# Fourteen products of the identity ahead of the first transposes

## The chip, the cores and the metric

The kernel runs on one core of one Trainium2 chip. The core has a matrix engine (TensorE, in the profile PE, with its weight loads as PEld), a vector engine (DVE), a scalar engine (ACT), a third engine for elementwise work (POOL) and an engine that only issues transfers (SP). They run side by side, each through its own list of instructions in order, and wait for each other by semaphores. The metric is the device time of one execution in microseconds (us). Lower is better.

## What is computed

Attention with normalised q and k, and behind it an MLP mixer. All data are float32. Batch 8, 12 heads, sequence 448, head dimension 64. The heads side by side make 768 channels.

```python
def rmsnorm(x, g):
    return x / np.sqrt(np.mean(x * x, axis=-1, keepdims=True) + 1e-06) * g

q_n, k_n = rmsnorm(q, g_q), rmsnorm(k, g_k)
scores = np.matmul(q_n, k_n.transpose(0, 1, 3, 2)) / np.sqrt(64)
attn = softmax(scores)                                # over the last axis
x = np.matmul(attn, v)                                # to (batch, seq, 768)

h = np.maximum(x.transpose(0, 2, 1) @ w_tok1, 0.0) @ w_tok2
u = x + h.transpose(0, 2, 1)                          # mixing along the sequence, 448 -> 256 -> 448
out = u + np.maximum(u @ w_ch1, 0.0) @ w_ch2          # mixing along the channels, 768 -> 1536 -> 768
```

## The kernel before

**Staging.** Heads are handled in pairs, six pairs to a batch, 48 in all. For a pair, q and k are loaded with the sequence on the partitions, squared on ACT (`square`, L1429), summed on DVE (`reduce`, L1445), the inverse root is found by Newton steps (`guess`, `newton`, L1467 to L1488), and DVE multiplies it in (`scale`, L1496). For the first pairs PE then turns q and k, so that the head dimension lies on the partitions (`turn_qk`, L429, a product with the identity as one operand), and ACT copies the turned blocks out of PSUM (L437 for k, L435 for q, which multiplies the gains in). `score` forms the scores of two pairs at a time (L455) and ACT takes their exponentials (L459). `values` multiplies with v (L528) and sums the rows with a matrix of ones (L508). Then follow, for each batch, the token mixing (L839, L846, L881) and the channel mixing (L971, L1001, L1050, L1067), for which the float weights are converted and combined on the chip (`weight_load` L222 and the conversions L345 to L379).

**Order.** Nothing is reordered by a scheduler: all engines have the order in which the program is written. Attention of a batch is interleaved with the mixing of the batch before it by lists of work items (`merge`, `place`, `run`).

**Start.** The class `Start` issues the loads of the first pairs, makes the identity on POOL (L1344, a memset and a select), normalises pairs 0 and 1, and decides on DVE, from the gains, whether the scores can get large (`large`, L1337). Then every engine loads that one number and takes a branch (L1533). Each arm of the branch holds the whole rest of the kernel, `whole`, once with shifted exponentials and once without; with these inputs it is the second. `whole` sets up its pools, issues loads of v, of weights and of pairs 4 and 5 on SP (L1204 to L1214), squares pairs 2 and 3 on ACT, and turns q and k of pairs 0 and 1: 16 transposes on PE in four groups, each group in a PSUM tile of its own.

**PSUM.** `ps_S` is a ring of four banks; `s_tile` takes the next. Turned blocks, scores and some sums use it. A tile waits until the tile four before it has been read. The identity `ident` is a 128x128 tile in `const`, which also serves later transposes.

The part of `whole` that orders the start:

```python
    pre.square(2, st)
    for p in range(2):
        for i in (1, 0):
            turn_qk(p, i)
        if not p:
            pre.square(3, st)
```

Of the kernel before, what the change touches and what calls it, by code (L numbers as in the profile page):

```python
# [83 lines left out]
def whole(ctx, tc, shifted, pre, q, k, v, g_q, g_k, moe_w_tok1, moe_w_tok2, moe_w_ch1, moe_w_ch2, out):  # L84


    nc = tc.nc
# [7 lines left out]
    P = 128  # L95
# [46 lines left out]
    ident, one_c, expo_c, g_t = pre.ident, pre.one_c, pre.expo_c, pre.g_t  # L142
# [9 lines left out]
    st = dict(pre.st)  # L152
    m_tile = lambda: ps_M.tile([P, 512], F32, name="m_ps", tag="M")
    s_tile = lambda name: ps_S.tile([P, 512], F32, name=name, tag="S")

    clock, pending = [0.0], []

# [1348 lines left out]
def kernel(  # L1506
# [26 lines left out]
    with tc.If(nc.values_load(large[0:1, 0:1], min_val=0, max_val=1,  # L1533
                              skip_runtime_bounds_check_because="a comparison's result") > 0) as arm:
        whole(tc, True, pre, *args)
    with arm.Else():
        whole(tc, False, pre, *args)
# [30 lines left out]
```

## Time and profile before

| | us |
|---|---|
| median of 3 runs | 1285.12 (1283.40 to 1287.99) |
| the profiled execution | 1283.78 |
| its span, first to last instruction | 1282.0 |
| PE busy | 1251.6 (98%) |
| DVE busy | 795.3 (62%) |
| ACT busy | 393.3 (31%) |
| POOL busy | 387.9 (30%) |
| PE before its first product | 12.77 |
| PE's longest later gap, at 28.15 | 3.27 |

All times in the profile count from the start of the span. A group of instructions has a line of the kernel, an engine, what is written and what is read, and a count. PE's products are pipelined, so one of them lasts longer than the step from one to the next. "PEldq", "ACTq" and so on are the sequencers of the engines, which take branches and semaphore waits; a wait's own record tells how long the sequencer stood in it. The releaser of an idle time is what ended it.

### The profile page before, as it was taken

How to read it: one execution, taken by the hardware profiler on the slowest of the kernel's cores; microseconds unless marked ns; L12 is line 12 of the kernel's file. 1: busy time of each engine (PE TensorE's matmuls, PEld its weight loads, DVE VectorE, ACT ScalarE, POOL GpSimd, SP SyncE). 2: the span in 40 equal slices, each digit the busy share in tenths (PEclk: the TensorE clock that was granted, in tenths of full speed). 3: DMA queues.
4: the chain of work that ended last, by engine and by line, in shares of the span. 5: the costliest groups of instructions: out<-in, count | busy, mean ns of one | idle time of the engine just before them, and what ended most of it. 6: DMA issues, size and time to landing. Idle time of an engine off the chain costs nothing.

```text
span 1282.0 us, 20022 instructions
## 1 busy us (share of the span) xinstructions
PE 1251.6 (98%) x7236; PEld 890.8 (69%) x7236; DVE 795.3 (62%) x1241; ACT 393.3 (31%) x785; POOL 387.9 (30%) x629
## 2 busy tenths in 40 slices
PE   4999999999999999999999999999999999999998
PEld 3444444457744487796778768885887867797998
DVE  6989778856664255864668356765558456554243
ACT  5663433223341144302443033311343024300210
POOL 1202552024995611331133122241122322131222
PEclk9999999999999999999999999999999999999999
DMA  7866595899899876695657867595766864386554
GB/s 174 192 188 175 154 233 147 208 241 250 239 237 229 195 165 169 142 249 117 159 161 160 207 142 185 131 222 123 190 159 141 236 134 138 115 208 146 185 175 103
DMA packets 490112, 228.37 MB, mean 178 GB/s; under 512 B 371860, under 2 KB 450580, under 8 KB 490004
## 3 DMA queue, kind: packets, MB, share of 16 engines
q1 hardware_dynamic: 483394, 214.25, 67.9%
q0 software_dynamic: 3584, 12.06, 3.1%
q8 instruction: 59, 0.97, 0.3%
q10 hardware_dynamic: 3026, 0.69, 0.3%
q14 instruction: 49, 0.40, 0.1%
HBM read 184.26 MB, written 42.66 MB: 177 GB/s over the span
## 4 chain that ended last, share of the span: by engine, by line
PE 86%; DVE 6%; DMA 2%; SPq 2%; issue 1%; ACT 1%; DVEq 0%; ACTq 0%
PE m_ps L1001 26%; PE m_ps L1067 21%; PE s_ps L455 9%; PE o_ps L528 8%; PE m_ps L881 5%; PE m_ps L971 5%; PE m_ps L1050 4%; PE m_ps L839 2%; PE t_ps L839 2%; PE d_ps L508 1%; DVE raw L346 1%; DVE raw L348 1%; DVE stage L379 1%; DMA raw<-wp 1%; PE m_ps L846 1%
## 5 line engine op out<-in xcount | busy, mean ns | idle before, releaser
L1067 PE MATMUL m_ps<-hb,unit 128*128 128x224 f32 x1440 | 277.2, 354 | 0.0
L1067 PEld LDWEIGHTS m_ps<-hb,unit 128*128 128x128 f32 x1440 | 270.9, 190 | 8.8 <-issue 7.7
L1001 PE MATMUL m_ps<-tu,unit 128*128 128x224 f32 x1008 | 201.6, 355 | 1.3 <-ACT r L1011 1.3
L1001 PEld LDWEIGHTS m_ps<-tu,unit 128*128 128x128 f32 x1008 | 189.1, 190 | 15.1 <-issue 9.2
L459 ACT ACTIVATE e<-s_ps 128x448 f32<-128x448 f32 x294 | 138.1, 549 | 177.7 <-PE s_ps L455 169.4
L1001 PE MATMUL m_ps<-uT,unit 128*128 128x224 f32 x756 | 151.2, 354 | 0.5 <-DVE hb L1007 0.5
L1001 PEld LDWEIGHTS m_ps<-uT,unit 128*128 128x128 f32 x756 | 142.2, 190 | 7.6 <-issue 4.6
L455 PE MATMUL s_ps<-qkT 64*64 64x448 f32 x1260 | 143.7, 545 | 0.8 <-ACT x L821 0.8
L528 PE MATMUL o_ps<-e,v 64*64 64x448 f32 x1148 | 129.4, 538 | 0.3 <-ACT uT L565 0.2
L496 DVE TENSOR_TENSOR es<-es,e 128x896 f32<-128x896 f32 x90 | 103.5, 1150 | 13.0 <-ACT e L459 7.6
L1007 DVE TENSOR_TENSOR hb<-m_ps,r 128x448 f32<-128x448 f32 x63 | 39.1, 621 | 108.5 <-POOL r L1007 57.0
L1007 POOL TENSOR_TENSOR hb<-r,r 128x448 f32<-128x448 f32 x21 | 24.0, 1143 | 243.6 <-ACT r L1023 243.6
L455 PEld LDWEIGHTS s_ps<-qkT 64*64 64x64 f32 x1260 | 44.9, 132 | 70.0 <-issue 59.9
L528 PEld LDWEIGHTS o_ps<-e,v 64*64 64x64 f32 x1148 | 45.2, 133 | 62.9 <-issue 59.2
L1475 POOL TENSOR_TENSOR nt<-rs 128x56 f32<-128x56 f32 (+1 forms) x54 | 21.9, 405 | 203.5 <-DVE rs L1467 200.7
L1008 ACT ACTIVATE hb<-hb 128x448 f32<-128x448 f32 x84 | 48.4, 577 | 101.1 <-DVE hb L1007 77.6
L881 PE MATMUL m_ps<-w_sb,h 128*128 128x448 f32 x192 | 75.2, 544 | 0.3 <-DVE uT L886 0.3
L1082 POOL TENSOR_TENSOR uT<-uT,r 128x448 f32<-128x448 f32 x42 | 51.4, 1240 | 78.5 <-DVE r L1082 46.7
L320 POOL TENSOR_TENSOR raw<-raw 128x128 f32<-128x128 f32 x128 | 64.4, 522 | 34.3 <-DMA raw<-wp 29.8
L1445 DVE TENSOR_REDUCE ms<-sq 128x28 f32<-128x896 f32 (+2 forms) x44 | 47.5, 1080 | 35.6 <-ACT sq L1432 28.6
L1007 DVE TENSOR_TENSOR r<-m_ps,r 128x448 f32<-128x448 f32 x42 | 26.1, 622 | 64.3 <-PE m_ps L1001 64.3
L886 DVE TENSOR_TENSOR uT<-uT,m_ps 128x448 f32<-128x448 f32 x48 | 29.3, 613 | 54.5 <-PE m_ps L881 54.5
(146 smaller groups left out, 1600.2 us busy)
## 6 DMA issues: line engine op xcount, KB each, us to landing
unit<-ws SPq DMA_DIRECT2D x267, 384.0 KB, 4.2
raw<-in_moe_w_ch_dram SPq DMA_DIRECT2D x72, 256.0 KB, 3.4
v<-in_v_dram SPq DMA_DIRECT2D x96, 112.0 KB, 3.9
out_dram<-turned SPq DMA_DIRECT2D x182, 56.0 KB, 1.9
xs<-xt SPq DMA_DIRECT2D x56, 168.0 KB, 4.7
qk_t<-in_q_dram SPq DMA_DIRECT2D x144, 56.0 KB, 3.5
qk_t<-in_k_dram SPq DMA_DIRECT2D x144, 56.0 KB, 3.7
x<-xs SPq DMA_DIRECT2D x42, 192.0 KB, 3.9
```

The lines of the kernel that those rows point to most:

```text
L320: nc.gpsimd.tensor_tensor(out=at[o], in0=at[x], in1=at[y], op=ALU.add if op == "+" else ALU.subtract)
L455: nc.tensor.matmul(out=pss[i][rows_of(i, a), 0:S], lhsT=qkT[h, 1, k * D:(k + 1) * D], rhs=qkT[h, 0, :], start=True, stop=True)
L459: nc.scalar.activation(out=e[:, i, :], in_=pss[i][:, 0:S], func=AF.Exp)
L496: nc.vector.tensor_tensor(out=es[:], in0=(es if k > 1 else st["e", t, 0])[:], in1=st["e", t, k][:], op=ALU.add)
L528: nc.tensor.matmul(out=st["o", p][a * D:(a + 1) * D, 0:S], lhsT=vt[rows, k * D:(k + 1) * D], rhs=e[rows, :], **kw)
L839: nc.tensor.matmul(out=st["t1", h][jc][:, 0:HC], lhsT=w1_sb[:, c, jc * P:(jc + 1) * P], rhs=st["x", b, h][:, :, c, :], start=start and c = ...
L881: nc.tensor.matmul(out=ps[:, 0:S], lhsT=st["h1", jc][:, cc * P:(cc + 1) * P], rhs=w2_sb[:, jc].rearrange("p c r -> p (c r)"), start=(jc == ...
L971: nc.tensor.matmul(out=ps, lhsT=a[:, o + 2 * half, :], rhs=natural(half * KF + t) if wide else u[:, half * KC + t, :], start=(t == 0 and h ...
L1001: nc.tensor.matmul(out=ps[:, j * HS:(j + 1) * HS], lhsT=w[:, t, j, :], rhs=m, start=(t == 0), stop=(t == KC - 1))
L1007: add = lambda e, o, x, y: e.tensor_tensor(out=o, in0=x, in1=y, op=ALU.add)
L1067: nc.tensor.matmul(out=ps[:, x * HS:(x + 1) * HS], lhsT=st["w"][:, tile_at % 6, :], rhs=hb[:, X_SLOT[f], i, :], start=(i == 0), stop=(i == 3))
L1082: e.tensor_tensor(out=get(out), in0=get(x_), in1=get(y), op=ALU.add if op == "+" else ALU.subtract)
```

## The change

In `whole`, right after the two PSUM helpers are defined, a tile of the ring `ps_S` is taken, and 14 products of the identity with itself are written into its first 128 columns. Each begins and ends its own sum, so each overwrites the one before. Nothing reads the tile. The products stand on PE behind the branch and in front of the first transposes; every later tile of the ring is one bank further on.

```diff
     m_tile = lambda: ps_M.tile([P, 512], F32, name="m_ps", tag="M")
     s_tile = lambda name: ps_S.tile([P, 512], F32, name=name, tag="S")
+
+    first_ps = s_tile("first_ps")
+    for _ in range(14):
+        nc.tensor.matmul(out=first_ps[:, 0:P], lhsT=ident[:, :], rhs=ident[:, :], start=True, stop=True)
 
     clock, pending = [0.0], []
```

Line numbers below the insertion are higher by four in the changed kernel.

## The prediction

> **What bounds the kernel now.** I read the page's busy shares first, then the clock, then the waits and the order of time in the first 32 us, because the change acts only there.
>
> ```profile
> span 1282.0 us, 20022 instructions
> ...
> PE 1251.6 (98%) x7236; PEld 890.8 (69%) x7236; DVE 795.3 (62%) x1241; ACT 393.3 (31%) x785; POOL 387.9 (30%) x629
> ...
> PE 86%; DVE 6%; DMA 2%; SPq 2%; issue 1%; ACT 1%; DVEq 0%; ACTq 0%
> ```
>
> TensorE (PE) bounds the kernel as a whole. But 98% is an average: the 30 us that PE is not busy are mostly two gaps at the start, 12.77 us before its first product and 3.27 us at 28.15. So the question is which wait ends last in the start. The order of time there, by engine:
>
> ```profile
> 12.77 3.22 PE L429 MATMUL t_ps<-ident,hb 112*128 112x112 f32 x16 [12.77 <-DVE hb L1496]
> ...
> 13.79 0.53 ACT L437 COPY hb<-t_ps 128x448 f32<-128x448 f32 x1 [1.36 <-PE t_ps L429]
> 14.54 0.63 ACT L435 ACTIVATE hb<-t_ps,g_t 128x448 f32<-128x448 f32 x1 [0.21 <-PE t_ps L429]
> ...
> 17.75 2.87 ACT L459 ACTIVATE e<-s_ps 128x448 f32<-128x448 f32 x6 [0.68 <-PE s_ps L455]
> ...
> 24.32 1.06 ACT L1429 ACTIVATE sq<-hb 112x1024 f32<-112x1024 f32 x1 [3.71 <-DMA hb<-in_k_dram]
> ...
> 27.39 0.43 DVE L345 TENSOR_SCALAR cv_sb<-raw 128x512 uint32<-128x512 uint32 x1 [2.08 <-DMA raw<-in_moe_w_tok_dram]
> ...
> 29.23 1.06 ACT L1429 ACTIVATE hb<-hb 112x1024 f32<-112x1024 f32 x1 [2.11 <-DMA hb<-in_k_dram]
> ...
> 31.41 0.82 PE L429 MATMUL t_ps<-ident,hb 112*128 112x112 f32 x3 [3.27 <-ACT e L459]
> ```
>
> In each line stand start, duration, instruction, and in brackets the idle time before it with its releaser. The reader is to see two things. PE's late first product is released by VectorE (DVE), which scales q and k. And at 24.32 and 29.23 ScalarE (ACT) waits for loads of k (3.71 and 2.11 us), DVE at 27.39 for a weight load (2.08 us). The chain of work that ended last runs through exactly this: from 14.93 to 26.28 it is SyncE issuing loads one behind the other (0.5 to 1.4 us a piece, 0.04 to 0.06 us apart), then a load of k landing at 29.15, then ACT, then PE at 31.41. None of those early loads waits for PE.
>
> When may PE start? The views of the branch line and of the first transposes' line say it:
>
> ```profile
> L1533 PEldq COMPARE_BRANCH  x1: 5624/5624/5624, 3.7 to 3.7; - x1
> ```
>
> ```profile
> L429 PEld LDWEIGHTS t_ps<-ident,hb x16: 182/231/231, 12.7 to 15.4; 112*128 112x128 f32 x16
> L429 PE MATMUL t_ps<-ident,hb x16: 394/394/421, 12.8 to 15.6; 112*128 112x112 f32 x16
> L429 PEldq EVENT_SEMAPHORE  x5: 51/51/3267, 9.3 to 13.8; - x5
> ```
>
> PE's branch ends at 3.66 + 5.62 = 9.28 us. From 9.34 PE stands 3.27 us in a semaphore wait, until 12.61. That is the hole into which the products go. The identity they read is complete at 4.14 (the select on POOL at 3.85, 0.29 us).
>
> And which clock does PE have? The row of granted clock shows full speed for the first slice, but that is no record: the same 16 transposes take 394 ns each at 12.8, 394 ns at 31.4 to 34.3, where the clock is recorded as 0.50, and 259 ns at 52.9, where it is 1.00. So the first transposes ran at half clock. The score products after them (L455) fall from 1006 ns at 15.9 to 573 at 17.5 and 536 later: full clock arrives near 17.5 us.
>
> **The Trainium skill.** "TensorE: Matmul & The Clock Gate", Part 1, says that the array starts at half clock and is given the full clock after a busy window of some 3.4 us, whose phase does not follow the kernel, and loses it after an idle one. The trace agrees: half until about 17.5, after 4.7 us of work from 12.77; full again after some 3.2 us of work at 31.4. Part 4 of that page says that transposes do not count as busy for this. The trace disagrees: in the stretch from 31.41 to 34.31 PE did nothing but transposes, and was at full clock after it. "Runtime: NRT & Kernel Launch", Instruction fetch mechanics, says that a taken branch must fetch its target before the engine goes on. That fits PE's 5.62 us; it is why the hole begins only at 9.3.
>
> **The change, part by part.** Nothing is removed. Both arms of the branch get 14 products; one arm runs.
>
> Added work. Half-clock transposes of 112 moving columns follow each other every 0.187 us (15 steps between 12.8 and 15.6). Mine have 128 columns: 0.187 x 128/112 = 0.213 us (an estimate); a weight load of 128 columns takes 0.18 to 0.23 us beside it. 14 x 0.213 = 2.99 us. Begun at 9.34 + 0.05, the last starts at 12.2 and drains at about 12.6. The first transposes are ready at 12.61 to 12.74. So the cost on the path is 0 to 0.1 us, hidden by DVE's scaling of q and k (L1496 from 11.87, the first piece ends near 12.5). Without that cover they would cost their 3.0 us. Bounds of the unshown pace: 14 x 0.10 = 1.4 us were the clock full (transposes at 52.9 go every 0.096 us), and 14 x 0.42 = 5.9 us if load and product did not overlap (largest product above, 421 ns). I take 3.0, because load and product overlap in every group above.
>
> Moved work: none. The transposes wait for the same scaling; the wait for POOL's identity goes to the first product; the fourth transposes' tile, which now takes the slot of the products' tile in the ring of four, waits for PE's own products, long done. Every later tile still waits for the fourth before it. No DMA, nothing on SP's, ACT's, POOL's or DVE's queues moves. POOL's memset at 15.49 follows the transposes, and matters to nobody near.
>
> What it brings. PE is busy from 9.4 instead of 12.77, so the full clock comes about 3.4 us earlier, between 12.8 and 16.2. Most that can be saved: PE's half-clock work from 12.77 to 17.5 is 4.7 us, so 2.4 us if all of it were at full clock and all on the path. On the path is less: scaling releases the transposes in four pieces of about 0.63 us, and ACT then copies, scales, squares (1.05 us) and copies again. With full clock at 14.1, the gain is ACT's wait of 0.68 us for the first scores; with full clock from the first transpose, 0.6 us at the second copy besides. So the first exponentials come 0.7 to 1.3 us sooner.
>
> Where that lead goes. ACT's next waits are for loads: 3.71 us at 24.32, and 2.11 at 29.23. An ACT that comes 0.7 to 1.3 us sooner waits so much longer. PE's gap at 28.15 grows from 3.27 to at most 4.6 us, and ends at 31.41 as before. DVE's wait at 27.39 grows the same way. Sum: +0 on the span of 1282.0, +0 on the profiled execution's 1283.78, which is 1.3 us under the median of 1285.12. I forecast the median unchanged: 1285.1 us.
>
> **Rivals.**
> (1) The lead survives: part of the next loads start sooner, or the unprofiled loads are quicker than those profiled. Against it: SP's chain has no wait for PE until 43 us. Most it can give is the 2.4 us above, so 1282.7; a fair middle is 1284. Even the most is 0.19%.
> (2) Slower: load and product don't overlap, 5.9 us. The last ends at 15.3 and the transposes start 2.6 us late. DVE, behind ACT's copies, is late by as much at 22.94, but its wait at 27.39 absorbs only 2.08; about 0.5 us is left, 1285.6. It decides once a product costs more than (12.74 - 9.39)/14 = 0.24 us, and shows in the time only above (3.35 + 2.08)/14 = 0.39 us. For 0.3% of the time, 3.9 us more, a product would have to cost 0.67 us. The 421 ns speak against it.
> (3) The change does nothing to the clock: the products end before a window is full and 0.1 to 0.4 us of idleness spoils it. Time the same, 1285.1, since the gain was to be lost anyway.
> (4) The longer gap at 28 us takes the clock down where it was not taken before. It was taken down before already (0.50 from 31.4). 1285.1 again.
>
> **How the numbers follow.** 0.3% is 3.9 us, about what a measurement of this kernel can tell from no change; the three runs before spread over 4.6, so a median of three may stray by some 1.5 (an estimate). No change, with (3) and (4): 63%, of which the stray puts 2 on either side. The lead survives: 16%, of which 4 read as faster. Slower by the products themselves: 8%, of which 2 read as slower. And 13% for what the sum can't see, a start that lands later loads and their waits differently through the other 1250 us: 8 faster, 5 slower. Faster 2 + 4 + 8 = 0.14, slower 2 + 2 + 5 = 0.09, same 0.77. Range: down to 1285.1 - 2.4 - 0.7 (half of the spread under the median) = 1282.0; up to 1285.6 plus the 2.9 of spread above the median = 1288.5.
>
> **What would show it.** Right: 14 products from 9.4, the first transposes still at 12.7 to 12.8, some or all of them at 259 ns, the first exponentials near 16.5 to 17.1; ACT's wait for k's load above 4 us; PE's second gap ending at 31.4 again. Wrong: transposes beginning after 13, or the third set of PE work (31.41) beginning earlier by as much as the first.

## The result, and the profile after

| | kernel before | changed kernel |
|---|---|---|
| median of 20 runs each | 1285.59 us | 1281.14 us |
| lowest to highest | 1280.32 to 1287.99 | 1278.02 to 1288.39 |
| ratio, 95% interval | | 0.9976 [0.9966, 0.9987] |
| profiled execution | 1283.78 | 1278.02 |
| its span | 1282.0 | 1276.2 |

The changed kernel is quicker by 0.24%, about 3 us. That is below the 0.3% named ahead as what can be told from no change, but the interval excludes no change. Against the three runs shown ahead, 0.9976 x 1285.12 = 1282.0 us, on the lower edge of the forecast range; the changed kernel's own median, 1281.14, lies below that edge.

**The start.** The order of time after, PE, ACT and VectorE:

```profile
9.42 5.84 PE L158 MATMUL first_ps<-ident 128*128 128x128 f32 x28 [9.42 <-DVE g_t L1369]
...
15.10 1.70 PE L433 MATMUL t_ps<-ident,hb 112*128 112x112 f32 x16
15.68 0.53 ACT L441 COPY hb<-t_ps 128x448 f32<-128x448 f32 x1 [1.88 <-PE t_ps L433]
...
18.53 0.56 ACT L463 ACTIVATE e<-s_ps 128x448 f32<-128x448 f32 x1
...
26.90 0.43 DVE L349 TENSOR_SCALAR cv_sb<-raw 128x512 uint32<-128x512 uint32 x1 [0.95 <-DMA raw<-in_moe_w_tok_dram]
...
29.11 1.06 ACT L1433 ACTIVATE hb<-hb 112x1024 f32<-112x1024 f32 x1 [2.33 <-DMA hb<-in_k_dram]
...
31.29 2.94 PE L433 MATMUL t_ps<-ident,hb 112*128 112x112 f32 x16 [2.48 <-ACT e L463]
```

The 14 products are 28 passes (a pass is one product record with its own weight load) and take 5.84 us, not 3.0. So they don't end in time: the transposes start at 15.10 instead of 12.77, 2.3 us late, although they now run at full clock (259 ns each, the granted clock recorded as full from 14.6). The first exponentials come at 18.53 instead of 17.75, later and not sooner. (The start differs between executions: with the kernel before they come at 17.75 to 18.19 in three profiles, with fourteen products at 17.52 to 18.96 in four.) Then the slack takes it all: VectorE's wait for the weight load shrinks from 2.08 to 0.95 us, and PE's second gap from 3.27 to 2.48. At 31 us PE is where it was (31.29 against 31.41). Product for product, both kernels then run within 0.03 us of each other from 35.8 to 214.

**Where the 5.8 us of the two spans come from.** From there on the lead of the changed kernel is 0.3 us at 293, 1.0 at 340 to 398, 5.77 at 449, and 5.76 at the end. So nearly all of it lies between 398 and 449. (Before 340 PE also had a shorter stand, at 335.28: 0.49 us for VectorE, L1007, which the changed kernel's profile does not have.) PE's order of time there, first before, then after:

```profile
426.23 0.92 PE L846 MATMUL m_ps<-x,w_sb 64*128 64x384 f32 x4
429.84 1.83 PE L846 MATMUL t_ps<-x,w_sb 64*128 64x384 f32 x4 [2.70 <-DMA x<-xs]
```

```profile
425.25 0.92 PE L850 MATMUL m_ps<-x,w_sb 64*128 64x384 f32 x4
426.00 1.06 PE L850 MATMUL t_ps<-x,w_sb 64*128 64x384 f32 x4
```

Before, PE stood 2.70 us for the second half of x of batch 2, which the kernel stores turned in DRAM and loads back. Then it ran at half clock: 1.83 us for four products that take 0.92; the clock is recorded at half for 3.41 us, from 430.56, which costs 1.7 us (an estimate: half of it). After, the load was in time. A stand at 427 us was in none of my steps. Whether it belongs to the change, or to one execution, is the question of the experiments.

The chain before leads from that stand back into SyncE's queue (SPq), which issues the load:

```profile
413.42 2.17 SPq L929
415.59 0.05 issue
415.64 0.43 SPq L788
416.07 0.05 issue
416.12 1.15 SPq L788
417.27 0.04 issue
417.32 4.45 DMA xs<-xt
...
423.39 6.31 DMA x<-xs
429.70 0.14 issue
429.84 1.83 PE t_ps L846 x4
```

In each line: start, duration, what. A load of weights (L929) stands for 2.17 us after its release by PE, three of the four stores of x wait behind it (L788), and only when they have landed can x be loaded. The same stretch of SyncE's queue, before and after:

```profile
412.21 0.32 SPq L788 DMA_DIRECT2D xs<-xt  x1
413.07 2.52 SPq L929 DMA_DIRECT2D unit<-ws  x1
415.64 3.36 SPq L788 DMA_DIRECT2D xs<-xt  x3
```

```profile
408.44 0.38 SPq L792 DMA_DIRECT2D xs<-xt  x1
408.96 2.55 SPq L933 DMA_DIRECT2D unit<-ws  x1
411.56 3.44 SPq L792 DMA_DIRECT2D xs<-xt  x3
```

The load of weights takes as long in the changed kernel, 2.55 us, although no release by PE falls into it there. What differs is that the whole queue is 4.1 us earlier at this load, where PE at 398 was only 1.0 us earlier. So the chain shows the way of the delay, and not yet its origin.

### The profile page after: what moved, and what is told of

Same layout as the page of the kernel before. It is cut to its first block, busy times and chain, and to the rows that moved or that the text cites. A ratio compares the mean times of both kernels' runs of the same rounds, so it can differ in the third digit from the quotient of the medians.

```text
span 1276.2 us, 20079 instructions
## 1 busy us (share of the span) xinstructions
PE 1252.3 (98%) x7264; PEld 891.4 (70%) x7264; DVE 797.8 (63%) x1241; ACT 392.8 (31%) x785; POOL 388.3 (30%) x629
## 4 chain that ended last, share of the span: by engine, by line
PE 89%; DVE 5%; DMA 2%; SPq 2%; ACT 1%; issue 1%; DVEq 0%; ACTq 0%
PE m_ps L1005 26%; PE m_ps L1071 22%; PE s_ps L459 9%; PE o_ps L532 9%; PE m_ps L885 6%; PE m_ps L975 5%; PE m_ps L1054 4%; PE m_ps L843 3%; PE t_ps L843 2%; PE d_ps L512 1%; PE m_ps L512 1%; DVE es L500 1%; DMA qk_t<-in_q_dram 1%; PE m_ps L850 1%; DVE raw L352 1%
```

## The experiments

Theories: (A) the busy start gains, by the clock or by its timing; (B) it is the bank shift of the PSUM ring; (C) it is where the program lies; (D) it is the luck of which executions had the stand at 427. Three groups of runs followed, and the kernel before ran in every one; medians of 58, 49 and 58 runs were 1284.49, 1284.99 and 1284.43 us.

| kernel | median us (runs) | ratio to before, 95% |
|---|---|---|
| changed kernel, again | 1281.26 (8) | 0.9970 [0.9956, 0.9983] |
| products in the other arm | 1282.86 (22) | 0.9991 [0.9980, 1.0001] |
| seven products | 1281.73 (19) | 0.9980 [0.9970, 0.9990] |
| one product | 1282.02 (22) | 0.9982 [0.9974, 0.9989] |
| before itself | 1283.78 (22) | 0.9987 [0.9978, 0.9996] |
| early x, no products | 1280.77 (12) | 0.9962 [0.9950, 0.9974] |
| early x, 14 products | 1279.50 (6) | 0.9945 [0.9925, 0.9966] |
| 28 products | 1283.79 (22) | 0.9988 [0.9976, 1.0000] |
| before itself, second | 1284.61 (14) | 1.0003 [0.9988, 1.0017] |
| changed kernel, third | 1280.72 (22) | 0.9973 [0.9962, 0.9984] |
| 14 products, ring not shifted | 1280.90 (12) | 0.9977 [0.9961, 0.9994] |
| 14 products, stores first | 1280.13 (21) | 0.9969 [0.9958, 0.9980] |

### Is it real? The same two kernels again

No edit in these four: the changed kernel twice, the kernel before twice.

> The changed kernel once more, beside the kernel before. If the 0.24% belong to the change, it is again 2 to 5 us quicker than before (ratio about 0.997). If they were the luck of which executions had a late load of x at 427 us, the ratio lies anywhere between 0.996 and 1.002.

> The kernel before itself, under another name. No theory moves it: ratio 1.000 within 0.1%. If it is 0.998, as the kernel with one product was, then the way the runs are taken makes that difference, and of the 0.24% only what lies beyond it belongs to the change.

> The kernel before itself once more, to set the others of this group against an equal count of runs: 0.998 to 1.000 of the kernel before, as it was 0.9987 the first time.

> The changed kernel a third time, on the chip of the kernel before itself. If it owes its gain to the change, its median lies 1.5 to 3.5 us under that of the kernel before itself; if to the choice of runs, within 0.7 us of it.

The changed kernel repeats: 0.9970 and 0.9973. The kernel before against itself gave 0.9987 and 1.0003. The first of these excludes 1 by a hair, against what I had expected, so differences of 0.1% must not be believed here, whatever their interval; 0.25% stands. In the last group, on one chip, the changed kernel lies 3.9 us under the kernel before itself (1280.72 against 1284.61). Theory D, chance alone, falls: the gain came in each of the three groups that held both kernels.

### Without executing them: the products in the arm not taken

```diff
-    first_ps = s_tile("first_ps")
-    for _ in range(14):
-        nc.tensor.matmul(...)
+    if shifted:
+        first_ps = s_tile("first_ps")
+        for _ in range(14):
+            nc.tensor.matmul(...)
```

> The 14 products stand only in the arm of the branch that is not taken: nothing more is executed than before, but the taken arm's program on TensorE begins 56 instructions further on. Theory 'where the program lies': as quick as the changed kernel, ratio about 0.997. Theory 'what is executed at the start' (busy TensorE, clock, delay): no change, ratio 1.000 within 0.1%.

0.9991, inside what the kernel before differed from itself. A shifted program of the taken arm, alone, doesn't give the gain. It doesn't clear theory C altogether: this program is 14 products shorter than the changed one, since the taken arm has none.

### Fewer and more products

```diff
-    for _ in range(14):
+    for _ in range(7):      # and 1, and 28
```

> Seven products, so 14 passes of 0.21 us, 3.0 us from 9.4: they end before the first transposes are ready at 12.7. Theory 'busy TensorE and clock': full clock is there as early as with fourteen and nothing is delayed, so at least as quick as the changed kernel, ratio 0.996 to 0.998. Theory 'the delay of the start moves the later loads': no delay, so as before, ratio 1.000.

> One product (0.4 us) keeps the tile in the ring of four, so each later tile of the ring lies one bank further on, and leaves out the long busy time and the delay. Theory 'the shift of the ring matters': as quick as the changed kernel, 0.997. Clock theory and delay theory: no change, 1.000 within 0.1%.

> Twenty-eight products: 56 passes of 0.21 us at half clock, fewer once the clock is full, at least 7 us. The first transposes begin near 17 to 21 instead of 12.8. By the prediction's slack (ACT 3.71 us at 24.3, VectorE 2.08 at 27.4) 2 to 6 us of it stay: 1287 to 1291. Theory 'any delay of the start is good for the later loads': as quick as the changed kernel or quicker.

PE's order of time at the start, with one, seven and 28:

```profile
9.86 0.77 PE L158 MATMUL first_ps<-ident 128*128 128x128 f32 x2 [9.86 <-DVE ms L1449]
13.19 1.20 PE L433 MATMUL t_ps<-ident,hb 112*128 112x112 f32 x5 [2.56 <-DVE hb L1500]
```

```profile
10.14 3.33 PE L158 MATMUL first_ps<-ident 128*128 128x128 f32 x14 [10.14 <-DVE ms L1449]
13.29 2.43 PE L433 MATMUL t_ps<-ident,hb 112*128 112x112 f32 x16
```

```profile
9.34 8.15 PE L158 MATMUL first_ps<-ident 128*128 128x128 f32 x56 [9.34 <-DVE g_t L1369]
17.33 1.70 PE L433 MATMUL t_ps<-ident,hb 112*128 112x112 f32 x16
```

Seven products do what I had thought fourteen would: 14 passes, then the transposes at 13.29 us, nearly all at full clock. (The kernel before has them at 12.77 in the profile shown, and at 13.57 and 13.42 in two others.) So the prediction's own account can be read here:

```profile
16.95 0.55 ACT L463 ACTIVATE e<-s_ps 128x448 f32<-128x448 f32 x1
24.45 1.06 ACT L1433 ACTIVATE sq<-hb 112x1024 f32<-112x1024 f32 x1 [4.03 <-DMA hb<-in_k_dram]
```

The first exponentials come 0.8 us sooner than before, within the forecast, and ACT then waits 4.03 us for k instead of 3.71. Seven give 0.9980, fourteen 0.9970 to 0.9977. So a gain seems to need no delay, and full clock without delay does not give more; but 0.9980 is not far from the 0.9987 of no change. One product leaves 2.6 us of idleness and the old half clock for the transposes (394 ns each), and has 0.9982; that can't be told from seven, and hardly from the first run of the kernel before against itself (0.9987). Twenty-eight delay the transposes by 4.6 us. I had expected 1287 to 1291, and 2 to 6 us to stay. It is 1283.79, as the kernel before itself: ACT's wait at 24.3 is gone, and the next one, for k at 31.04, holds:

```profile
24.31 1.06 ACT L1433 ACTIVATE sq<-hb 112x1024 f32<-112x1024 f32 x1
25.28 1.96 ACT L463 ACTIVATE e<-s_ps 128x448 f32<-128x448 f32 x4
31.04 1.06 ACT L1433 ACTIVATE hb<-hb 112x1024 f32<-112x1024 f32 x1 [3.81 <-DMA hb<-in_k_dram]
```

So in this profile the start has at least 4.6 us of slack ahead of that wait, more than I gave it. The load of k lands later here (31.04, against 29.23 before and 29.67 to 30.30 in four others with one product, the products in the other arm or no change); whether the late start has a part in that is not shown. And the gain doesn't grow with the products: it is gone at 28. A busier PE or an earlier full clock can't be the whole of it (theory A in its simple form).

### The ring

```diff
     first_ps = s_tile("first_ps")
+    for _ in range(3):
+        s_tile("spare_ps")
     for _ in range(14):
```

> Fourteen products as in the changed kernel, but four tiles of the ring are taken for them, so that every later tile lies in the same bank as before. Theory 'the shift of the ring gains': the gain is gone, equal to the kernel before itself within 0.7 us. Theory 'the busy start or the program's place gains': as the changed kernel.

0.9977 with every later tile in its old bank, and 3.7 us under the kernel before itself of that group (1280.90 against 1284.61): the gain is not the ring's (theory B falls).

### The stand at 427 taken away

```diff
         x, xs = x_tile(b, half), st.pop(("xs", b, half))...
+        if (b, half) == (2, 1):
+            xs = wp2[:].rearrange("p m n -> (p m) n")[0:KC * S]...
...
-            ... (2, 1): (0.0, 0.25, 6.0)
+            ... (2, 1): (0.0, 0.25, 0.0)
```

The same edit without and with the products; the second half of x of that batch is then other data. The loads of x also go ahead of its four stores in SyncE's queue, so the edit does more there than take the stand away.

> The kernel before, but the second half of x of batch 2 is loaded some 6 us sooner and from other data of the same size (the reordered weights), so that TensorE never stands at 427 us for it; the output is wrong for that batch. Theory 'the change only shortens the stand at 427 us': 2 to 5 us quicker than before, ratio 0.996 to 0.998. If the stand is not what differs: ratio 0.999 to 1.000.

> The same edit of the load in the changed kernel; it leaves out the same data. Theory 'the change only shortens the stand at 427 us': equal to the kernel with the early load and without the products, within 0.1%. Theory 'the start itself gains': 2 to 4 us quicker than that one.

```profile
429.03 0.92 PE L848 MATMUL m_ps<-x,w_sb 64*128 64x384 f32 x4
429.78 0.81 PE L848 MATMUL t_ps<-x,w_sb 64*128 64x384 f32 x4
```

This is the kernel without products: the stand is gone, and the time falls from 1284.99 to 1280.77, by 4.2 us. Against the kernel before itself of that group (1283.78) it is 3.0 us. None of the 12 runs took more than 1282.80, where 14 of the 22 of the kernel before itself took over 1283. So what this edit takes away, the stand above all, costs the kernel before some 3 to 4 us in its middle run, not only in the profiled one. With the products the same edit gives 1279.50. The two kernels are 1.3 us apart now, with six runs on one side, where they are 3.7 apart with the stand in place (1280.72 against 1284.43). By these medians about two thirds of the gain goes through the stand. That is a rough estimate: medians of runs drawn again from the 12 and the 6 put the 1.3 us anywhere from -0.8 to 2.8 (95%), so the stand may carry all of the gain, or only a quarter.

Eleven profiles, one execution each, point the same way. I set the start of the same product against the kernel before's profile: of the product at 115 us, of that at 398, and of the last. The last column is the time from the product at 398 to SyncE's first store of that half of x.

| profile | at 115 | 115 to 398 | 398 to end | stand at 427 | 398 to first store |
|---|---|---|---|---|---|
| before | 0 | 0 | 0 | 2.70 | 14.00 |
| before itself, first | +1.89 | +0.21 | -2.73 | 1.40 | 12.49 |
| before itself, second | +2.50 | +0.15 | -2.06 | 2.34 | 13.20 |
| products in the other arm | +1.00 | +0.71 | -3.01 | 0.73 | 11.50 |
| changed | +0.03 | -1.01 | -4.78 | none | 11.21 |
| changed, again | +1.90 | -0.82 | -3.27 | 0.93 | 11.85 |
| changed, third | +0.72 | -1.18 | -4.47 | none | 11.32 |
| ring not shifted | +2.59 | +0.95 | -3.47 | 0.65 | 11.69 |
| one product | +0.51 | +0.41 | -3.63 | 0.82 | 12.25 |
| seven products | +1.85 | -1.21 | -3.08 | none | 11.18 |
| 28 products | +2.11 | +0.41 | +3.14 | 2.05, then 1.32 | 15.19 |

At 115 us the four without executed products are at +1.35 on average, the four with fourteen at +1.31: the start gains nothing, as predicted. What spreads this column is the clock after PE's second gap: it is recorded at half for 3.41 us in the profiles at 0 to +1.00, and for 6.82 us in those at +1.85 to +2.59, with products and without. (With 28 products it is 3.41.)

The stretch from 398 to the end differs by 2.0 us (-1.95 against -4.0), that from 115 to 398 by 0.8. These are means of four executions that spread as widely, and one product has -3.63; they are a hint, no proof. The last two columns go together more firmly: no stand where the first store follows within 11.32 us, 0.65 to 0.93 at 11.50 to 12.25, then 1.40, 2.34 and 2.70, and at 15.19 two stands. So the stand goes with how far SyncE's queue is behind PE by then: 11.18 to 11.85 us with seven or fourteen products, 11.50 to 14.00 with one or none executed. The half clock does not always follow: after the stands of 1.40 and 2.34 us none is recorded.

### The four stores of x, one behind the other

The chain before shows three stores of x behind a load of weights, and I took that load to wait there for PE. In the changed kernel the stores can go ahead of it.

```diff
-            ... (2, 1): (0.0, 0.25, 6.0)
+            ... (2, 1): (0.0, 0.0, 6.0)
```

> The changed kernel, with the four stores of the turned second half of x of batch 2 issued one behind the other, ahead of the weight load that now stands between the first and the other three and waits for TensorE there (2.5 us on SyncE's queue). If the stand at 427 us is what is left to gain, x lands 2 to 3 us sooner, the stand is gone from the trace, and the time falls to 1279 to 1280.5, with fewer runs above 1283 than the changed kernel; if not, it equals the changed kernel within 0.7 us.

SyncE's queue in this version:

```profile
408.38 6.20 SPq L792 DMA_DIRECT2D xs<-xt  x4
414.67 1.42 SPq L933 DMA_DIRECT2D unit<-ws  x2
417.17 1.43 SPq L801 DMA_DIRECT2D x<-xs  x3
418.65 1.24 SPq L804 DMA_DIRECT2D x<-xs  x2
```

The four stores stand together, but the 2.5 us have not gone: the second store, now in the place of the load of weights, takes 2.56 us itself, from 409.06. So my reading of that load was wrong: the 2.5 us belong to whatever follows the first store, in all three profiles, and not to a wait for PE. The stores end at 414.6, against 415.0 in the changed kernel. The last load of x is issued by 419.9, against 425.7 in the kernel before and 421.5 in the changed one. PE has no stand there, but neither has it in two of three profiles of the changed kernel.

The median is 1280.13, 0.6 us under the changed kernel of the same group, which their intervals don't separate; this meets my "if not" (within 0.7 us) as well as the other case. The highest of 21 runs is 1282.8, where the changed kernel reached 1284.6. It beats the kernel before by 0.31% [0.20%, 0.42%]; that it beats the changed kernel too is not shown. In the kernel without products the order was not tried.

## Why the prediction was right and wrong

**Right: the verdict within 0.3%, and where the lead of the start would go.** The forecast "+0 on the span" held for its own ground: the loads of k and of weights release ACT and VectorE at 27 to 29 us, with 28 products ACT still waits 3.81 us for k (until 31.04), and at 115 us the kernels with and without fourteen products are together. With seven products the rest of the account can be seen as well: sooner exponentials, a longer wait for k. That the measured time fell on the edge of the range was luck: what took it there is in no step of the sum. The edge itself had a slip: half of the spread under the median is (1285.12 - 1283.40)/2 = 0.86 us, not 0.7.

**Wrong: the pace of the products.** The step "14 x 0.213 = 2.99 us" had the pace right and the count wrong. At half clock a pass takes 0.21 us, but a float32 product is two passes and only a transpose is one: 28 records for 14 products. The page before had it:

```profile
L1067 PE MATMUL m_ps<-hb,unit 128*128 128x224 f32 x1440 | 277.2, 354 | 0.0
```

These are 1440 records, where six batches x 15 forms x 8 calls make 720 products. The price was 5.84 us, my upper bound 5.9, and the transposes began at 15.10, past the 13 that I had named as a sign of being wrong. So rival (2) happened, by its amount (2.6 us late forecast, 2.3 measured) though not by its cause (load and product do overlap), and its absorption too.

**Wrong: "the first exponentials near 16.5 to 17.1".** They came at 18.53, following from that count; with seven products at 16.95. That the clock would be full for the first transposes was right: 259 ns instead of 394.

**Wrong: "Sum: +0".** The measured change is -0.24% to -0.30% in three groups of runs. What failed is the silent step that nothing changes after 31 us. The 13% that I gave to "a start that lands later loads and their waits differently" is the case that came, with a smaller size than its 0.3%. Its place is, by the runs, mainly the stand for x at 427 us, which goes with a few microseconds on SyncE's queue. I read the waits of the first 60 us and never asked which later wait ends just in time.

**Open: how the products reach 427.** From 35.8 to 214 us the two profiles run in step; PE's times part at 218.5. At 376.56 SyncE's next load of weights has stood 6.5 us for a transfer that POOL issues (ws<-raw, L310), in the changed kernel 4.9 us, and is issued 2.8 us later than there; why is not shown. It is not the ring's bank, not chance alone, and hardly the delay of the transposes (seven have none, 28 have more and no gain). The program's place is not excluded: it was moved only in part. Nor is an interplay of the clock's windows with the transfers: over 50 runs of the changed kernel the recorded half-clock time is 6.3 us per run, over 165 runs of the kernel before 8.9 (twice the missing share of the mean granted clock, times the span). But half clock followed the stand in the profile before, so this may be effect and not cause, and 2.6 us at half clock cost 1.3 at most. Nor does it go with the gain: with the products in the other arm it is 6.3 us, with 28 products 6.0, and neither gained. Products of the same number placed where they meet no idle PE, or at the end, were not tried.

## What to carry to other kernels

Filling an idle engine ahead of its first work is worth only what the next wait for a load lets through; follow the lead to that wait before counting it. Count instructions from the trace's own records: a float32 product is two passes on PE here. And where a change of nothing moves the time by 0.2%, look for the one wait in the middle that is met just in time: here it cost some 3 to 4 us, more than the 2.4 us that the edit at the start could bring. And before calling a load in the queue a wait for another engine, look at its duration where that engine has long released it: here it was 2.5 us either way.

## What the runs showed that was not expected

- A float32 product of 128 x 128 with 128 columns is two weight loads and two product records, 0.21 us a pass at half clock; the transposes of float32 blocks are one each.
- The kernel before against itself gave 0.9987 [0.9978, 0.9996] in one group and 1.0003 [0.9988, 1.0017] in another: the first interval excludes 1, though nothing differed.
- A 2.70 us stand on PE came with 4.78 us between the two profiles from 398 us to the end; in part since the clock was half for 3.41 us after the stand: 1.83 us for four products that took 0.92 before it. After a stand of 2.34 us in another profile the clock stayed full.
- The instruction behind the first store of x stood for 2.5 us on SyncE's queue (2.52, 2.55, 2.56), whether it was a load of weights or the next store.
